# Spaces of 32 and 64 bytes between the late weight tiles of two mixture layers, in a matmul-bound kernel

## The chip, the cores and the metric

One core of one Trainium2 chip. The metric is the time of one execution on the device in microseconds (us); the times of several runs are given by their median.

## What is computed

Decayed linear attention over 2 x 8 heads x 768 positions, then a dense layer pair with g(h) = h * cos(h), then a mixture of eight experts with one expert for each token. Cut to what matters:

```python
x = np.ascontiguousarray(attn_out.transpose(0, 2, 1, 3)).reshape(B * S, H * D)   # 1536 x 512
h = x @ w_in                                                                     # 512 -> 2048
x = (h * np.cos(h)) @ w_out                                                      # 2048 -> 512
...
e_idx = np.argmax(x @ w_gate, axis=1)
for e in range(8):
    h = np.maximum(x[mask] @ w1[e], 0.0)                                         # 512 -> 1024
    out[mask] = gate_w[mask, None] * eom[mask, e, None] * (h @ w2[e])            # 1024 -> 512
```

## The kernel before, in words

All matrix products of the two layers run as products of float32r parts: a weight is split into a high and a low half (`hi`, `lo`), an activation likewise, and three products (high by high, high by low, low by high) are added in PSUM. The 1536 tokens are six blocks of 256. The hidden width of the dense layer is cut into eight pieces p = 0..7 of 256; an expert's into four.

The stages that matter here, with their lines:

- **First layer, `first`.** `mm_duo` (L511) multiplies two blocks at once: 12 matmuls with 512 moving columns for each half f of a piece; the weights `w_in` are the stationary operand and the tokens move. `mm_l1` (L499) does one block: 24 matmuls of 256 columns for a piece.
- **Second layer, `second`.** `mm_duo2` (L520) and `mm_l2` (L538): 12 matmuls of 512 columns each; here the activations `g` are stationary and the weights `w_out` move.
- **Order of the steps.** First come pieces 0 and 1 of blocks 0 to 2, beside the attention. Then for every p = 0..7 a step of the pair of blocks 3 and 4 in two halves and of block 5: L511, L520, L511, L520 or L538, L499 and so on. Then p = 2..7 for the pair of blocks 0 and 1 (12 half steps, L511 and L520), at last p = 2..7 of block 2 (L499 and L538).
- **Experts 0 and 1** are done in halves of 128 rows (`h_l1` L955, `h_l2` L982, both 512 columns, weights moving). **Experts 2 to 7** take 208 rows: `mm_rows` (L527 with 416 columns and L528 with 208, eight such pairs for a piece, weights stationary), `c_cols` (L904 with 416 and L906 with 208, eight pairs, weights stationary); expert 7 ends with L538.

**Where the weights lie.** `w_tile` gives the tile of a piece. Pieces 0 and 1 of `w_in` are the tile `wa01`; pieces 0 and 1 of `w_out` lie in the pool `wb`; pieces 2 to 7 lie in the pools `w2a` (`w_in`) and `w2b` (`w_out`), one tile of 8192 bytes per partition for each piece, kept for the whole kernel. The experts use the same tiles again: expert e takes places 0 to 3 or 4 to 7 of both pools (`place`), w1 in the first and w2 in the second. A pool gives out its addresses in the order in which its tags are first asked for: w7 first (by the loop on `spot`), then w2 to w6.

As built, a tile's first byte within 512 bytes is:

| tile | before | with the change |
|---|---|---|
| `wa01` (pieces 0, 1 of w_in), raw tiles | 320 | 320 |
| tokens `xs01`, `xs2`; activations `g`; pieces 0, 1 of w_out | 0 | 0 |
| w_in / w1 at places 7, 2, 3, 4, 5, 6 | all 0 | 32, 64, 96, 128, 192, 224 |
| w_out / w2 at places 7, 2, 3, 4, 5, 6 | all 0 | 224, 256, 288, 320, 352, 384 |

All slices of a weight tile that a matmul reads start at multiples of 512 bytes from the tile's start, so the table holds for each matmul's weights. PE, DVE and ACT run in the order of the program text (a manual schedule).

**The two small pools.** `sc` holds the row scales of the experts (`row_scale`, L745 to L767), `xt1` the single numbers of a rarely taken path at the end. Before, both are opened beside the weight pools and stay. `rt` and `xr` (routing) are closed in `routed` (L1003), where `rows` takes their place.

Of the kernel before, what the change touches and what calls it, by code (L numbers as in the profile page):

```python
# [8 lines left out]
F32 = mybir.dt.float32  # L9
F32R = mybir.dt.float32r  # L10
# [18 lines left out]
def kernel(  # L29
# [27 lines left out]
    NP = DFF // 256  # L57
# [18 lines left out]
    wb_p = ctx.enter_context(tc.tile_pool(name="wb", bufs=1))  # L76
# [56 lines left out]
    HP = 2  # L133
# [39 lines left out]
    pools = {}  # L173

    def w_load():
        i = nxt["load"]
        if i >= len(order) or (order[i][0] == "w1" and not pools.get("cleared")):
            return
        nxt["load"] += 1
        key = order[i]  # L180
        src = src_of[key[0]](*key[1:])
        words = key[0] in ("in", "out")
        pool, tag = (xt_p, "xt") if pools.get("spare") and i % 5 < 3 else (raw_p, "raw")
        if not pools.get("spare") and nxt["used"] < nxt["free"]:
            pool, tag = xt_p, "xt"
            nxt["used"] += 1
        if "raw2" in pools and i % 2:
            pool = pools["raw2"]
        if i in spot:
            t = spot[i]  # L190
        else:
            t = pool.tile([128, 1024], I32 if words else F32, tag=tag, name="raw")
            if pool is raw_p:
                in_raw.append(key)
        dst = t
        if len(src.shape) == 3:
            dst = t.rearrange("p (k f) -> p k f", k=src.shape[1])
        nc.sync.dma_start(out=dst, in_=src)
        raw_t[key] = t

    def w_tile(a, p, name):
        if a and p < HP:
            return wa01[:, p]
        pool = wb_p if p < HP else pools["w2a" if a else "w2b"]
        return pool.tile([128, 2, 1024], F32R, tag=f"w{p}", name=name)

    half_done, high_done = [], []
    spot, in_raw, used = {}, [], set()
# [13 lines left out]
    def word_parts():  # L222
# [7 lines left out]
        if f == 0:  # L230
            wt[name, p] = w_tile(name == "in", p, f"w_{name}_{p}")
# [343 lines left out]
    def behind(get, others):  # L575
        for x in others:
            tc.add_manual_dep(
                get.ins, x.name, mybir.DependencyInfo(mybir.DependencyClass.Sync, mybir.DependencyReason.DATA),
                reason="reads the scattered rows")
# [207 lines left out]
    def h_rows(t):  # L787
        for e in range(HALVED):
            if t == 0:
                r = cv_p.tile([128, ROW], F32, tag="x", name="hrows")  # L790
            else:
                if e == 0:
                    pools["h1"] = pools["rows"].tile([128, HALVED, ROW], F32, tag="rows", name="hrows")
                r = pools["h1"][:, e, :]
            r0 = e * CAP + t * 128
            behind(nc.sync.dma_start(out=r, in_=xs_d[r0:r0 + 128, :]), sent)
            rows[e, t] = r.unsqueeze(1)
# [16 lines left out]
    def c_rows(e):  # L814
        if e >= E:
            return
        t = pools["rows"].tile([128, 2, ROW], F32, tag="rows", name="rows")[0:HL]
        get = nc.sync.dma_start(
            out=t, in_=xs_d[(e + 1) * CAP - LIM:(e + 1) * CAP, :].rearrange("(t p) f -> p t f", p=HL))
        behind(get, sent)  # L820
        rows[e, 2] = t
# [17 lines left out]
    def c_high():  # L839
        i = nxt["split"]  # L840
        if i >= len(order):
            return
        nxt["split"] += 1
        key = order[i]
        r = raw_t.pop(key)
        t = w_tile(key[0] == "w1", place(*key), "w_" + "_".join(str(z) for z in key))
        nc.scalar.copy(out=t[:, 0, :], in_=r)  # L847
        low_due.append((t, r, key))
        wt[key] = t
# [145 lines left out]
    def totals():  # L995
        cps = side_tile([128, 512], "cps")
        nc.tensor.matmul(cps[:, 0:E], lhsT=ones, rhs=accoh, start=True, stop=True)
        nc.vector.tensor_add(out=cnt, in0=cps[:, 0:E], in1=skip[:, 0, :])
        nc.vector.tensor_scalar(more, cnt, float(127 - CAP), 0.0, ALU.add, ALU.max)
        nc.vector.tensor_scalar(more, more, 7, None, ALU.arith_shift_right)  # L1000
        nc.vector.tensor_reduce(out=most, in_=more, op=ALU.max, axis=AX.X)

    def routed():  # L1003
        totals()
        for c in reversed(rt_cms):
            c.__exit__(None, None, None)
        pools["rows"] = ctx.enter_context(tc.tile_pool(name="rows", bufs=2))
        h_rows(1)
        c_rows(HALVED)
        pools["spare"] = True  # L1010
        for _ in range(3):
            w_load()
# [101 lines left out]
    pools["side"] = ctx.enter_context(tc.tile_pool(name="ps_side", bufs=2, space=PSUM))  # L1114
    for nm, key in (("w2a", "w2a"), ("w2b", "w2b")):
        pools[key] = ctx.enter_context(tc.tile_pool(name=nm, bufs=1))
    pools["sc"] = ctx.enter_context(tc.tile_pool(name="scp", bufs=2))
    pools["xt1"] = ctx.enter_context(tc.tile_pool(name="xt1", bufs=1))
    pools["rt"], pools["xr"] = [c.__enter__() for c in rt_cms]
    WHOLE = NSB + 4 * HALVED  # L1120
    for z in range(4):
        if z % 2 == 0:
            t = pools[("w2a", "w2b")[z // 2]].tile([128, 2, 1024], I32, tag=f"w{NP - 1}", name="spot")
        spot[nxt["load"] + z] = t[:, z % 2]
    phase = tc.manual_schedule(engines={
# [142 lines left out]
    h_l1(H + 2, 1)  # L1268
    h_turn(H + 1)
    routed()  # L1270
    h_l2(H)
    convert_early(2)
# [44 lines left out]
    for i in range(WHOLE + 2, len(steps) + LAG):  # L1317
        e, p = divmod(i - WHOLE, EP)
# [73 lines left out]
    with tc.If(over > 0):  # L1392
# [13 lines left out]
        for e in range(E):  # L1406
            pos = pools["xt1"].tile([128, 1], F32, tag="pos", name="pos")
            nc.vector.tensor_copy(out=pos, in_=lane)
            n = nc.values_load(
                more[0:1, e:e + 1], min_val=0, max_val=limit, skip_runtime_bounds_check_because="counts of rows")  # L1410
# [33 lines left out]
```

## Time and profile before

| | |
|---|---|
| time, median of 3 runs | 522.54 us (522.42 to 523.0) |
| the profiled execution: its time | 523.34 us |
| its span, first to last instruction | 521.6 us |
| mean granted TensorE clock | 0.996 |
| PE / DVE / ACT / POOL busy | 98% / 66% / 61% / 19% of the span |
| DMA, mean over the span | 162 GB/s |

Matmuls overlap in the pipeline and their ends are modelled, so the duration of one says little; what a stream of them costs is read from the starts of its groups in the timeline: from the start of one group to the start of the next one.

### The profile page before, as it was taken

How to read it: one execution, taken by the hardware profiler on the slowest of the kernel's cores; microseconds unless marked ns; L12 is line 12 of the kernel's file. 1: busy time of each engine (PE TensorE's matmuls, PEld its weight loads, DVE VectorE, ACT ScalarE, POOL GpSimd, SP SyncE). 2: the span in 40 equal slices, each digit the busy share in tenths (PEclk: the TensorE clock that was granted, in tenths of full speed). 3: DMA queues.
4: the chain of work that ended last, by engine and by line, in shares of the span. 5: the costliest groups of instructions: out<-in, count | busy, mean ns of one | idle time of the engine just before them, and what ended most of it. 6: DMA issues, size and time to landing. Idle time of an engine off the chain costs nothing. (4 is left out here: it accounts for less than half of the span.)

```text
span 521.6 us, 8979 instructions
## 1 busy us (share of the span) xinstructions
PE 511.3 (98%) x3428; PEld 448.9 (86%) x3428; DVE 346.7 (66%) x672; ACT 317.3 (61%) x556; POOL 101.2 (19%) x129
## 2 busy tenths in 40 slices
PE   7989999999999999999999999999999999999995
PEld 7879988888888888887777888878889999999993
DVE  5897874577667566545554677756378888788740
ACT  3566655577666666655454665456577776777630
POOL 3454111132322323200102301311000011010111
PEclk9999999999999999999999999999999999999998
DMA  8999952232322423603912253658379777876311
GB/s 202 231 271 276 296 185 80 83 121 82 116 87 80 122 80 93 198 33 119 319 63 83 84 167 120 216 194 246 127 226 299 243 236 237 252 236 202 110 30 35
DMA packets 81938, 84.56 MB, mean 162 GB/s; under 512 B 41468, under 2 KB 61948, under 8 KB 81118
## 3 DMA queue, kind: packets, MB, share of 16 engines
q1 hardware_dynamic: 79646, 77.48, 49.3%
q0 software_dynamic: 2240, 6.42, 3.3%
q8 instruction: 29, 0.48, 0.4%
q14 instruction: 23, 0.19, 0.1%
HBM read 66.70 MB, written 17.65 MB: 162 GB/s over the span
## 5 line engine op out<-in xcount | busy, mean ns | idle before, releaser
L520 PE MATMUL acc<-w_out,g 128*128 128x512 f32 x336 | 82.3, 394 | 0.0
L520 PEld LDWEIGHTS acc<-w_out,g 128*128 128x128 f32 x336 | 61.7, 188 | 13.4 <-issue 1.2
L554 DVE SCALAR_TENSOR_TENSOR a<-a,t 128x512 f32<-128x512 f32 x48 | 34.6, 722 | 57.8 <-ACT a L551 57.8
L854 DVE TENSOR_TENSOR w_w<-raw,w_w 128x1024 fp32r<-128x1024 f32 x55 | 66.7, 1217 | 6.8 <-ACT w_w L847 6.7
L550 ACT ACTIVATE t<-h,quarter 128x512 f32<-128x512 f32 x48 | 33.0, 688 | 49.3 <-PE h L511 27.8
L847 ACT CAST w_w<-raw 128x1024 fp32r<-128x1024 f32 x55 | 57.6, 1054 | 2.2 <-DMA raw<-in_moe_w_dram 2.2
L538 PE MATMUL acc<-w_out,g 128*128 128x512 f32 x240 | 58.5, 394 | 0.0
L538 PEld LDWEIGHTS acc<-w_out,g 128*128 128x128 f32 x240 | 44.4, 188 | 9.6 <-issue 0.2
L904 PE MATMUL acc<-g,w_w 128*128 128x416 f32 x160 | 50.0, 371 | 0.0
L557 ACT ACTIVATE t<-a 128x512 f32<-128x512 f32 x48 | 30.3, 632 | 32.0 <-DVE a L554 32.0
L558 DVE TENSOR_TENSOR a<-t,h 128x512 f32<-128x512 f32 x48 | 33.0, 688 | 23.1 <-ACT t L557 21.0
L780 POOL DMA_INDIRECT out_dram<-y,who x16 | 16.1, 1005 | 148.2 <-ACT y L777 144.9
L527 PE MATMUL hw<-xs,w_w 128*128 128x416 f32 x144 | 44.7, 369 | 0.0
L561 ACT CAST g<-a 128x512 fp32r<-128x512 f32 x48 | 29.8, 621 | 23.8 <-DVE a L558 23.4
L562 DVE TENSOR_TENSOR g<-a,g 128x512 fp32r<-128x512 f32 x48 | 33.2, 692 | 16.5 <-ACT g L561 14.5
L906 PE MATMUL acc<-g,w_w 128*128 128x208 f32 x160 | 41.3, 258 | 0.0
L528 PE MATMUL hw<-xs,w_w 128*128 128x208 f32 x144 | 37.2, 258 | 0.0
L499 PEld LDWEIGHTS h<-xs,w_in 128*128 128x128 f32 x288 | 35.9, 191 | 1.1 <-issue 0.4
L499 PE MATMUL h<-xs,w_in 128*128 128x256 f32 x288 | 36.7, 284 | 0.0
L551 ACT ACTIVATE a<-t,magic 128x512 f32<-128x512 f32 x48 | 34.8, 725 | 1.6
L511 PE MATMUL h<-wa,w_in 128*128 128x512 f32 x144 | 35.2, 393 | 0.0
L268 POOL TENSOR_TENSOR w_out<-x,w_out 128x512 fp32r<-128x512 f32 x16 | 23.7, 1481 | 57.5 <-ACT w_out L262 56.8
(179 smaller groups left out, 1020.1 us busy)
## 6 DMA issues: line engine op xcount, KB each, us to landing
raw<-in_moe_w_dram SPq DMA_DIRECT2D x63, 512.0 KB, 4.5
raw<-in_moe_w_in_dram SPq DMA_DIRECT2D x14, 512.0 KB
raw<-in_moe_w_out_dram SPq DMA_DIRECT2D x14, 512.0 KB, 3.2
xs_d<-zrow SPq DMA_DIRECT2D x16, 266.0 KB, 4.3
x_d<-xrow SPq DMA_DIRECT2D x6, 532.0 KB
k<-in_k_dram SPq DMA_DIRECT2D x12, 256.0 KB, 6.8
q<-in_q_dram SPq DMA_DIRECT2D x12, 256.0 KB, 6.5
v<-in_v_dram SPq DMA_DIRECT2D x12, 256.0 KB
```

Of the source, the lines that this page charges most:

```text
L499: nc.tensor.matmul(h[:, f * n:(f + 1) * n], lhsT=wA(key, ws, kk, f), rhs=x[:, xx, kk, :], start=(z == 0), stop=(z == 3 * KD - 1))
L511: nc.tensor.matmul(h, lhsT=wA(key, ws, kk, f), rhs=x[:, :, xx, kk, :], start=(z == 0), stop=(z == 3 * KD - 1))
L520: nc.tensor.matmul(accs[t], lhsT=gf[:, gs, t * 128:(t + 1) * 128], rhs=wB(key, ws, f), start=(first and n == 0), stop=(last and n == 2))
L527: nc.tensor.matmul(h, lhsT=wA(key, 0, kk, f), rhs=x[:, kk], start=(kk == 0), stop=False)
L528: nc.tensor.matmul(h[:, 0, :], lhsT=wA(key, 1, kk, f), rhs=x[:, kk, 0, :], start=False, stop=(kk == KD - 1))
L538: nc.tensor.matmul(accs[t][0:m], lhsT=g[:, gs, f, t * m:(t + 1) * m], rhs=wB(key, ws, f), start=(first and n == 0), stop=(last and n == 5))
L551: nc.scalar.activation(out=a, in_=t, func=AF.Identity, bias=magic)
L554: nc.vector.scalar_tensor_tensor(out=a, in0=a, scalar=MAGIC, in1=t, op0=ALU.subtract, op1=ALU.subtract)
L847: nc.scalar.copy(out=t[:, 0, :], in_=r)
L854: nc.vector.tensor_sub(out=t[:, 1, :], in0=r, in1=t[:, 0, :].bitcast(F32))
L904: nc.tensor.matmul(acc, lhsT=wB(("w2", e, p), 0, f)[:, cols], rhs=g[:, :, f, :], start=(p == 0 and f == 0), stop=False)
L906: nc.tensor.matmul(acc[:, 0, :], lhsT=wB(("w2", e, p), 1, f)[:, cols], rhs=g[:, 0, f, :], start=False, stop=(p == EP - 1 and f == 1))
```

## The change

It asks the two pools for a small tile named `space` before the tile of a piece: 8 or 16 floats (32 or 64 bytes) per partition. Nothing reads or writes these tiles. So that all still fits, `sc` and `xt1` are opened after the routing pools are closed.

```diff
+    SHIFT_A = {7: 8, 2: 8, 3: 8, 4: 8, 5: 16, 6: 8}
+    SHIFT_B = {2: 8, 3: 8, 4: 8, 5: 8, 6: 8}
+    shifted = set()
+
+    def shift(a, p):
+        n = (SHIFT_A if a else SHIFT_B).get(p, 0)
+        if n and (a, p) not in shifted:
+            shifted.add((a, p))
+            pools["w2a" if a else "w2b"].tile([128, n], F32, tag=f"s{p}", name="space")
+
     def w_tile(a, p, name):
         if a and p < HP:
             return wa01[:, p]
-        pool = wb_p if p < HP else pools["w2a" if a else "w2b"]
-        return pool.tile([128, 2, 1024], F32R, tag=f"w{p}", name=name)
+        if p < HP:
+            return wb_p.tile([128, 2, 1024], F32R, tag=f"w{p}", name=name)
+        shift(a, p)
+        return pools["w2a" if a else "w2b"].tile([128, 2, 1024], F32R, tag=f"w{p}", name=name)
...
         pools["rows"] = ctx.enter_context(tc.tile_pool(name="rows", bufs=2))
+        pools["sc"] = ctx.enter_context(tc.tile_pool(name="scp", bufs=2))
+        pools["xt1"] = ctx.enter_context(tc.tile_pool(name="xt1", bufs=1))
         h_rows(1)
...
-    pools["sc"] = ctx.enter_context(tc.tile_pool(name="scp", bufs=2))
-    pools["xt1"] = ctx.enter_context(tc.tile_pool(name="xt1", bufs=1))
...
         if z % 2 == 0:
+            shift(z == 0, NP - 1)
             t = pools[("w2a", "w2b")[z // 2]].tile([128, 2, 1024], I32, tag=f"w{NP - 1}", name="spot")
```

On every engine and every queue the instructions and their order stay as they were; no instruction is added or taken away on them. What moves is a wait. On DVE, at the first expert's row scales (`h_scale(0, 0)`; `hrows` are that expert's rows, `ng` the first of the small tiles of `sc`, DMASW the queues of the indirect writes), there stood before:

```order
422 L854 TENSOR_TENSOR w_w_1_2_3866<-raw,w_w_1_2_3866 128x1024 [waits DMAHW5_49,Activation_49]
423 L972 TENSOR_TENSOR hg<-hT,hg 128x512 [waits Activation_49]
424 L854 TENSOR_TENSOR w_w_1_3_3887<-raw,w_w_1_3_3887 128x1024 [waits DMAHW0_49,Activation_49]
425 L755 TENSOR_SCALAR ng<-hrows 128x1 [waits DMAHW6_49]
426 L763 TENSOR_SCALAR sm<-sm 128x1 [waits Activation_49]
427 L764 TENSOR_SCALAR ez<-ez 128x1 [waits Activation_49]
```

and with the change:

```order
422 L866 TENSOR_TENSOR w_w_1_2_3877<-raw,w_w_1_2_3877 128x1024 [waits DMAHW5_49,Activation_49]
423 L984 TENSOR_TENSOR hg<-hT,hg 128x512 [waits Activation_49]
424 L866 TENSOR_TENSOR w_w_1_3_3898<-raw,w_w_1_3_3898 128x1024 [waits DMAHW0_49,Activation_49]
425 L767 TENSOR_SCALAR ng<-hrows 128x1 [waits DMASW3_49,DMASW2_49,DMAHW4_49,DMASW1_49,DMAHW6_49,DMASW0_49,Pool_49]
426 L775 TENSOR_SCALAR sm<-sm 128x1 [waits Activation_49]
427 L776 TENSOR_SCALAR ez<-ez 128x1 [waits Activation_49]
```

The wait for the last indirect writes of routing, which stood two row scales later, now stands at this first one, since `sc` lies where a buffer of `xr` lay. The same wait moves on ACT to the table load ahead of the first `ex`, and on POOL to the first write of rows to `out`.

## Rows read from the trace of the kernel before

**Rows 1.** The page, part 1: span, and PE's busy time.

```profile
span 521.6 us, 8979 instructions
PE 511.3 (98%) x3428; PEld 448.9 (86%) x3428; DVE 346.7 (66%) x672; ACT 317.3 (61%) x556; POOL 101.2 (19%) x129
```

**Rows 2.** Windows: stretch and length, busy time (instructions) of each engine, granted clock.

```profile
100.00:217.00 117.00, 117.00 (x599) 100.12 (x598) 77.83 (x129) 82.35 (x129) 32.69 (x24) 1.00 0.31 98
400.00:500.00 100.00, 100.00 (x691) 99.54 (x689) 81.25 (x159) 68.94 (x152) 8.02 (x8) 1.00 0.69 213
```

**Rows 3.** Timeline, PE, piece 6 of blocks 3 to 5: start us, length us, group.

```profile
186.13 2.91 PE L520 MATMUL acc<-w_out,g 128*128 128x512 f32 x12
188.88 2.88 PE L511 MATMUL h<-xs,w_in 128*128 128x512 f32 x12
191.60 2.88 PE L520 MATMUL acc<-w_out,g 128*128 128x512 f32 x12
194.32 2.88 PE L511 MATMUL h<-xs,w_in 128*128 128x512 f32 x12
197.04 2.88 PE L538 MATMUL acc<-w_out,g 128*128 128x512 f32 x12
199.76 3.04 PE L499 MATMUL h<-xs,w_in 128*128 128x256 f32 x24
202.63 0.63 PE L520 MATMUL acc<-w_out,g 128*128 128x512 f32 x2
```

**Rows 4.** Timeline, PE, piece 1 of the same blocks: weights in wa01.

```profile
97.84 2.96 PE L511 MATMUL h<-xs,wa 128*128 128x512 f32 x12
100.64 2.99 PE L499 MATMUL h<-xs,wa 128*128 128x256 f32 x24
103.47 0.86 PE L520 MATMUL acc<-w_out,g 128*128 128x512 f32 x3
```

**Rows 5.** Timeline, PE, first steps of blocks 0 and 1: tokens in wa01 move.

```profile
221.88 2.93 PE L511 MATMUL h<-wa,w_in 128*128 128x512 f32 x12
224.64 2.93 PE L520 MATMUL acc<-w_out,g 128*128 128x512 f32 x12
227.41 2.93 PE L511 MATMUL h<-wa,w_in 128*128 128x512 f32 x12
230.18 1.09 PE L538 MATMUL acc<-w_out,g 128*128 128x512 f32 x4
```

**Rows 6.** Groups by line, PE, whole span: names, count, busy us, mean ns.

```profile
L520 PE MATMUL acc<-w_out,g 128*128 128x512 f32 x336 | 82.3, 394 | 0.0
L511 PE MATMUL h<-wa,w_in 128*128 128x512 f32 x144 | 35.2, 393 | 0.0
L499 PE MATMUL h<-xs,w_in 128*128 128x256 f32 x288 | 36.7, 284 | 0.0
L982 PE MATMUL acc<-w_w,hg 128*128 128x512 f32 x96 | 24.0, 399 | 0.0
L527 PE MATMUL hw<-xs,w_w 128*128 128x416 f32 x144 | 44.7, 369 | 0.0
```

**Rows 7.** Timeline, PE, experts: eight pairs with w_w, then eight with wa.

```profile
405.50 0.37 PE L527 MATMUL hw<-xs,w_w 128*128 128x416 f32 x1
...
407.91 0.52 PE L803 MATMUL xps<-ident,rows 104*128 104x104 f32 x4
...
431.51 0.37 PE L527 MATMUL hw<-xs,wa 128*128 128x416 f32 x1
...
433.93 0.37 PE L904 MATMUL acc<-g,w_w 128*128 128x416 f32 x1
```

**Rows 8.** Line L847, ACT's writes of weight tiles: ns min/median/max, first and last start.

```profile
L847 ACT CAST w_w<-raw x55: 1031/1054/1077, 237.3 to 491.7; 128x1024 fp32r<-128x1024 f32 x55
L847 ACT CAST wa<-raw x8: 1031/1054/1074, 293.2 to 458.9; 128x1024 fp32r<-128x1024 f32 x8
```

**Rows 9.** Lines L796, L758 and L755: SP's row loads, ACT's table load, DVE's queue.

```profile
L796 SPq DMA_DIRECT2D hrows<-xs_d x4: 338/382/428, 331.9 to 357.1; - x4
L758 ACT ACT_TABLE_LOAD  x1: 1283/1283/1283, 358.1 to 358.1; - x1
L755 DVEq EVENT_SEMAPHORE  x3: 49/50/50, 372.7 to 372.9; - x3
```

## The prediction

> **What bounds the kernel now.** I read the page's busy times first. PE is busy for 511.3 of 521.6 us and DVE, the next, for 346.7 [rows 1]. The windows say the same of the stretches in which the late weight tiles are used: from 100 to 217 us and from 400 to 500 us PE is busy all the time and its clock is granted in full, while DVE and ACT have room [rows 2]. So the time of these stretches is the sum of the spacings of PE's matmuls, and a change of addresses counts if it changes a spacing. Only the timeline shows that: the start of a group to the start of the next one, over the matmuls in the group.
>
> The reader should then compare groups of the same line whose operands lie differently. In the steps of blocks 3 to 5 with pieces 2 to 7 every operand starts at 0 within 512 bytes. There a group of twelve 512-column matmuls takes 191.60 - 188.88 = 2.72 us, and so do the next three groups [rows 3], 226.7 ns for each matmul. Only the L520 group right behind the 24 small matmuls of L499 takes 2.75 (186.13 to 188.88), and the L499 group 2.87 (199.76 to 202.63). One step earlier in the program's order the same line L511 with the same tokens reads its stationary weights from `wa01`, at 320 within 512 bytes: 97.84 to 100.64, 2.80 us, 3% more; but L499 from the same tile takes 2.83 (100.64 to 103.47), 1.4% less [rows 4]. And where the tokens that move lie in `wa01` and the weights at 0, L511 takes 221.88 to 224.64, 2.76 us, and the L520 group behind it, with both operands at 0, does not fall back to 2.72 but takes 2.77; so does the pair after it, 227.41 to 230.18 being 2.77 [rows 5]. **So the relative place of the two operands does show in the spacing**, by a few hundredths of a microsecond for a group, both ways, and a group out of step leaves the next one slower. All-zero offsets give the shortest group of twelve that these rows hold.
>
> The rule that speaks against any effect: the Trainium skill, SBUF — State Buffer, section "SBUF: two separate sides", says that TensorE has its own ports and never waits on anyone, and TensorE: Matmul & The Clock Gate, "Step-by-step: what each phase is for", that loading the next weights takes no read bandwidth from the running matmul because there are two read ports. By that rule the sum below is 0. The trace disagrees: 2.80 against 2.72 us for one line with one tile exchanged.
>
> **The change, part by part.** *Adds and removes:* no instruction. The `space` tiles are never touched.
>
> *Blocks 3 to 5, pieces 2 to 7: six steps.* Each has two L511 groups, two L520 groups, one L538 group and one L499 group. L511 gets stationary weights off 0: 2.72 to 2.80, as in rows 4, +0.16 for two. L520 and L538 get moving weights off 0: the nearest row is a moving operand off 0 and what follows it, 2.77 [rows 5]; before they take 2.75 + 2.72 + 2.72 = 8.19 [rows 3], after 3 x 2.77 = 8.31, +0.12. L499: 2.87 to 2.83, -0.04. Together +0.24 a step, **+1.44 us** for six. I take these values because the rows are of the same lines; offset 320 is only one offset, and the new ones (32 to 384) are not in the trace. From below: only L511 pays, +0.12 a step, 0.72; from above: all five groups of twelve pay what L511 pays, 0.08, or (5 x 2.80) - (4 x 2.72 + 2.75) - 0.04 = 0.33 a step, 2.0.
>
> *Blocks 0 and 1: 24 groups of twelve* (144 matmuls of L511, as many of L520 [rows 6]). They run at 2.76 to 2.77 already, out of step because `wa01` moves [rows 5]. The new weights change one unlucky relation into another: **0**, with 0.04 a group either way (up to 2.80, or back to the aligned 2.72), 24 x 0.04 = 0.96 on both sides.
>
> *Block 2: six L499 groups and six L538 groups.* 6 x -0.04 = -0.24. The L538 groups stand behind other work and are not at 2.72 throughout; between 0 and +0.05 each I take 0.02, +0.12. Together **-0.1**.
>
> *Experts 0 and 1.* The moved places hold 12 of 16 tiles, so 72 of the 96 matmuls of L982 [rows 6] and as many of L955: twelve groups of twelve, again often restarted, +0.02 each: **+0.2** (0 to 0.6).
>
> *Experts 2 to 7.* Eight pairs of L527 and L528 take 405.50 to 407.91, 2.41 us, with weights at 0, and 431.51 to 433.93, 2.42, with weights at 320 [rows 7]. 144 / 8 = 18 such groups move [rows 6], and 15 groups of L904 and L906 (20 pieces, 5 of them in places that stay): 33 x 0.01 = **+0.3**. Nothing shows the pairs with other offsets; bounds are L499's -1.4% and L511's +3% of 2.41, or -0.03 and +0.07 a group: -1.0 to +2.3.
>
> *ACT, DVE and POOL write and read the tiles.* ACT's conversion takes 1054 ns in the median into the tiles at 0 and 1054 ns into `wa01` at 320 [rows 8]: nothing. Off 0 or not, these engines also have time left in both stretches [rows 2].
>
> *The moved wait.* The first row scale now waits for the last indirect writes. The row loads of SP at L796 wait for the same writes, and the last of them is issued at 357.1; ACT's table load, the first that would wait now, starts at 358.1 anyway [rows 9]. So the landing is covered by 1.0 us, and **0** is paid; what the queue spends on more semaphores (DVE: three of 50 ns, now earlier [rows 9]) is at most 0.2 us and only if PE waits for the hidden activations queued behind it on ACT. Without that cover the expert's first result and the next `hg` would come late by what the writes lack.
>
> Sum: 1.44 + 0 - 0.1 + 0.2 + 0.3 = **+1.8 us**. The profiled execution took 523.34 us, 0.80 over the median of the runs shown and 1.74 more than its span; it would go to 525.1. On the median, 522.54 + 1.8 = **524.3 us**. A measurement here can tell some 0.2% from no change, 1.05 us, so the bounds are 521.5 and 523.6. This case's own range is 523.6 to 526.0: the terms of the first stage between 0.7 and 2.0, the rest up to half their upper bounds.
>
> **The rivals.**
>
> *Spread offsets let the streams pass each other: faster.* Place: all matmuls with a moved operand. For it speaks L499, where a weight tile off 0 gains 1.4% [rows 3, 4]: with the operands at the same offset the loads and the stream may ask for the same place in turn, and 226.7 ns need not be the least possible spacing. Price at the same 1.4%: 30 groups of twelve in the first stage, 24, 6 and 12 in the others, 72 x -0.04 = -2.9; L499 12 x -0.04 = -0.5; expert pairs 33 x -0.03 = -1.0; in all -4.4, 518.1 us. If half the offsets are lucky, -2.2: **520.3 us**. It decides once the 72 groups, now 2.74 on average, come under 2.73, which with L499 is -1.2. Against it: neither L511 nor L520 shows a single group under 2.72, and the one stationary offset seen costs 3%.
>
> *Nothing, or gains and losses cancel: 522.5 us.* The new offsets give L499's gain (12 x -0.04 = -0.5, and the same from some others) against L511's loss. The two read ports of the Trainium skill, TensorE: Matmul & The Clock Gate, "Step-by-step: what each phase is for", would give the same time without any gain or loss. The changed offsets are multiples of 32 bytes; if only 320 were special and these offsets read like 0, all but L499 would stay at rows 3.
>
> *The moved wait bites: slower, by another way.* If the last writes land a microsecond later than before, ACT's table load and what is queued behind it shift by the same, and PE would wait for `hg`: under 1 us, 523 to 523.5. The cover of 1.0 us speaks against it [rows 9].
>
> *The change does not do what it says.* Excluded as built: the offsets are those asked for, the order of every engine is the same.
>
> **How the numbers follow.** The first stage slower as in rows 4 and 5: 0.44. Faster: 0.33, since one line of three gains by an offset and most new offsets are unseen. No change that can be told, with the late wait in it: 0.23. The range must reach both sides: 520.2, where the faster case has half its price, to 526.0, the upper end of the likeliest; about one in ten is left out below (the full price) and one in ten above.
>
> **What would show it.** In the profile after, the timeline of PE for pieces 2 to 7 of blocks 3 to 5: right if the L511 groups take 2.76 to 2.80 and the L520 groups 2.75 to 2.80, with L499 near 2.83 and a step 0.15 to 0.3 longer than the 16.5 us from one L520 group behind L499 to the next (186.13 to 202.63 [rows 3]). Wrong, to the fast side, if these groups show 2.70 or less; wrong to no change if they stay at 2.72. The table load of ACT should still start within 0.2 us of the conversion before it, and ACT's and DVE's durations should be the same. If the steps of blocks 0 and 1 move by more than 0.04 a group, the term that I set to 0 was the one that decided.

## The result and the profile after

The changed kernel takes 525.37 us in the median of five runs (524.99 to 526.95), the kernel before 523.0 (522.42 to 523.16) beside it: ratio 1.0054, 95% interval 1.0037 to 1.007. It is slower. The forecast was 524.3 us against a median of 522.54, which is a ratio of 1.0034, with 523.6 to 526.0 as the range of the slower case. Since the median of before moves between 523.0 and 523.7 from one comparison to another, ratios are compared below, not medians.

The page's first part of the kernel after, as [rows 1]:

```profile
span 523.6 us, 8978 instructions
PE 514.6 (98%) x3428; PEld 448.8 (86%) x3428; DVE 346.6 (66%) x672; ACT 317.3 (61%) x556; POOL 101.6 (19%) x129
```

PE's busy time grew by 3.3 us and its count did not change; DVE, ACT and POOL have the times of before. PE still has no gap to speak of, so the added time lies in the spacing of its matmuls.

To see where, cut both executions at the same matmuls: piece 1 of blocks 3 to 5 (L511, now L523), its piece 2, the first step of blocks 0 and 1, block 2's first, the first of experts 0 and 1, the expert pair of [rows 7], and the start of the last matmul. Windows of the kernel before (stretch and length, busy time and instructions of each engine, granted clock, DMA share, GB/s):

```profile
97.84:122.88 25.04, 25.04 (x134) 21.44 (x132) 16.51 (x27) 16.78 (x27) 6.10 (x4) 1.00 0.26 79
122.88:221.88 99.00, 99.00 (x506) 84.82 (x504) 64.30 (x107) 68.55 (x108) 27.87 (x21) 1.00 0.35 110
221.88:294.61 72.73, 72.68 (x359) 57.40 (x358) 37.02 (x89) 39.06 (x61) 6.82 (x10) 1.00 0.32 117
294.61:338.46 43.85, 43.85 (x293) 38.21 (x291) 32.06 (x70) 25.57 (x38) 9.26 (x12) 1.00 0.50 160
338.46:405.50 67.04, 67.04 (x373) 57.49 (x372) 43.03 (x97) 42.40 (x79) 7.26 (x7) 1.00 0.67 216
405.50:515.00 109.50, 109.50 (x729) 106.11 (x728) 80.26 (x159) 69.16 (x153) 11.01 (x11) 1.00 0.60 184
```

The same stretches of the kernel after:

```profile
97.26:122.30 25.04, 25.04 (x134) 21.45 (x133) 16.50 (x27) 16.79 (x27) 6.12 (x4) 1.00 0.23 81
122.30:222.68 100.38, 100.38 (x505) 84.59 (x504) 64.30 (x107) 68.51 (x108) 27.79 (x21) 1.00 0.33 108
222.68:296.01 73.33, 73.30 (x358) 57.43 (x357) 37.01 (x89) 39.08 (x61) 6.94 (x10) 1.00 0.32 116
296.01:339.93 43.92, 43.92 (x292) 37.96 (x291) 32.04 (x70) 25.52 (x38) 9.63 (x12) 1.00 0.49 160
339.93:407.38 67.45, 67.45 (x373) 57.53 (x372) 43.00 (x97) 42.47 (x79) 7.14 (x7) 1.00 0.66 214
407.38:517.09 109.71, 109.71 (x729) 106.13 (x728) 80.26 (x159) 69.29 (x153) 11.02 (x11) 1.00 0.60 183
```

The second column is the length. It grows by 0, 1.38, 0.60, 0.07, 0.41 and 0.21 us, 2.67 together, with PE busy throughout and its clock granted in full in both. The stretch ahead of 97.84, the attention, is 0.58 us shorter, so that the last matmul starts 515.00 to 517.09, 2.09 later. No matmul before that mark reads a tile that moved, and in the runs below that share this (the first five) the same matmul starts anywhere from 96.85 to 98.42 us. These 0.58 us are within that scatter, and a single span is worth no more than that. The stretches behind the mark repeat far better: in the first two runs below, which lose nothing, they add up to 417.08 and 417.09 us, before to 417.16.

PE's timeline after, piece 6 of blocks 3 to 5 (start us, length us, group), which answers to [rows 3]:

```profile
186.28 2.97 PE L532 MATMUL acc<-w_out,g 128*128 128x512 f32 x12
189.09 2.95 PE L523 MATMUL h<-xs,w_in 128*128 128x512 f32 x12
191.88 2.98 PE L532 MATMUL acc<-w_out,g 128*128 128x512 f32 x12
194.70 2.96 PE L523 MATMUL h<-xs,w_in 128*128 128x512 f32 x12
197.50 2.98 PE L550 MATMUL acc<-w_out,g 128*128 128x512 f32 x12
200.31 2.96 PE L511 MATMUL h<-xs,w_in 128*128 128x256 f32 x24
203.11 2.94 PE L532 MATMUL acc<-w_out,g 128*128 128x512 f32 x12
```

From one start to the next the groups take 2.81, 2.79, 2.82, 2.80, 2.81 and 2.80 us, where before they took 2.75, 2.72, 2.72, 2.72, 2.72 and 2.87. The step is 203.11 - 186.28 = 16.83 us against 16.50. In this step the weights of piece 6 of `w_in`, which stand, lie at 224 within 512 and those of piece 5 of `w_out`, which move, at 352 (the second layer runs one piece behind the first); in what follows such tiles are written `w_in_6` and `w_out_5`. Not every tile off 0 costs so much; the same timeline where `w_out_2` moves, which lies at 256:

```profile
136.22 2.91 PE L532 MATMUL acc<-w_out,g 128*128 128x512 f32 x12
138.97 2.97 PE L523 MATMUL h<-xs,w_in 128*128 128x512 f32 x12
141.77 2.44 PE L532 MATMUL acc<-w_out,g 128*128 128x512 f32 x10
```

L532 takes 2.75 here, what it took at 0. In blocks 0 and 1, as [rows 5]:

```profile
222.68 2.91 PE L523 MATMUL h<-wa,w_in 128*128 128x512 f32 x12
225.43 2.95 PE L532 MATMUL acc<-w_out,g 128*128 128x512 f32 x12
228.21 2.91 PE L523 MATMUL h<-wa,w_in 128*128 128x512 f32 x12
```

L523 takes 2.75 and no longer 2.76, L532 2.78 and no longer 2.77. `wa01` and `w_in_2` explain the first: `wa01` moves from 320 and `w_in_2` stands at 64, and 320 - 64 = 256. So two hints stand in this profile: it is the difference of the two addresses that counts, not each by itself, and 256 counts as 0.

The engines that write and read the tiles, and the moved wait: line L859 (L847 before, [rows 8]), and ACT's timeline around its table load [rows 9].

```profile
L859 ACT CAST w_w<-raw x55: 1032/1056/1069, 238.1 to 493.7; 128x1024 fp32r<-128x1024 f32 x55
L859 ACT CAST wa<-raw x8: 1035/1052/1081, 294.5 to 460.8; 128x1024 fp32r<-128x1024 f32 x8
```

```profile
358.59 1.06 ACT L859 CAST w_w<-raw 128x1024 fp32r<-128x1024 f32 x1
359.68 1.28 ACT L770 ACT_TABLE_LOAD   x1
```

The conversions last what they lasted, and the table load starts 0.03 us after the conversion ahead of it ends (358.59 + 1.06 = 359.65). The moved wait delays nothing.

### The profile page after: what moved, and what is told of

The parts are those of the page before. It is cut to its first block, busy times and chain, and to the rows that moved or that the text cites. A ratio compares the mean times of both kernels' runs of the same rounds, so it can differ in the third digit from the quotient of the medians.

```text
span 523.6 us, 8978 instructions
## 1 busy us (share of the span) xinstructions
PE 514.6 (98%) x3428; PEld 448.8 (86%) x3428; DVE 346.6 (66%) x672; ACT 317.3 (61%) x556; POOL 101.6 (19%) x129
## 5 line engine op out<-in xcount | busy, mean ns | idle before, releaser
L532 PE MATMUL acc<-w_out,g 128*128 128x512 f32 x336 | 83.2, 396 | 0.0
L532 PEld LDWEIGHTS acc<-w_out,g 128*128 128x128 f32 x336 | 61.7, 188 | 14.2 <-issue 1.2
L566 DVE SCALAR_TENSOR_TENSOR a<-a,t 128x512 f32<-128x512 f32 x48 | 34.6, 722 | 59.1 <-ACT a L563 59.0
L550 PE MATMUL acc<-w_out,g 128*128 128x512 f32 x240 | 59.0, 396 | 0.0
L859 ACT CAST w_w<-raw 128x1024 fp32r<-128x1024 f32 x55 | 57.6, 1053 | 2.2 <-DMA raw<-in_moe_w_dram 2.2
L550 PEld LDWEIGHTS acc<-w_out,g 128*128 128x128 f32 x240 | 44.4, 188 | 10.1 <-issue 0.2
L511 PEld LDWEIGHTS h<-xs,w_in 128*128 128x128 f32 x288 | 35.4, 188 | 1.2 <-issue 0.4
L511 PE MATMUL h<-xs,w_in 128*128 128x256 f32 x288 | 36.2, 281 | 0.0
L523 PE MATMUL h<-wa,w_in 128*128 128x512 f32 x144 | 35.4, 394 | 0.0
L523 PE MATMUL h<-xs,w_in 128*128 128x512 f32 x144 | 35.4, 395 | 0.0
```

The lines of the kernel that those rows point to most:

```text
L511: nc.tensor.matmul(h[:, f * n:(f + 1) * n], lhsT=wA(key, ws, kk, f), rhs=x[:, xx, kk, :], start=(z == 0), stop=(z == 3 * KD - 1))
L523: nc.tensor.matmul(h, lhsT=wA(key, ws, kk, f), rhs=x[:, :, xx, kk, :], start=(z == 0), stop=(z == 3 * KD - 1))
L532: nc.tensor.matmul(accs[t], lhsT=gf[:, gs, t * 128:(t + 1) * 128], rhs=wB(key, ws, f), start=(first and n == 0), stop=(last and n == 2))
L550: nc.tensor.matmul(accs[t][0:m], lhsT=g[:, gs, f, t * m:(t + 1) * m], rhs=wB(key, ws, f), start=(first and n == 0), stop=(last and n == 5))
L566: nc.vector.scalar_tensor_tensor(out=a, in0=a, scalar=MAGIC, in1=t, op0=ALU.subtract, op1=ALU.subtract)
```

## Theories and experiments

**Theory.** The spacing of PE's matmuls is set by the address of the weights that stand less the address of the rows that move, within 256 bytes. At a difference of 0 a group of twelve 512-column matmuls falls into the shortest spacing; at any other that the changed kernel has it is 1.3 to 3.5% longer. **Rivals:** the later pools and the moved wait cost something by themselves; it is the variety of offsets that counts; it is the distance from 0 within 512 bytes of either tile that counts.

### Only the later pools (e1_late_pools)

```diff
-    SHIFT_A = {7: 8, 2: 8, 3: 8, 4: 8, 5: 16, 6: 8}
-    SHIFT_B = {2: 8, 3: 8, 4: 8, 5: 8, 6: 8}
+    SHIFT_A = {}
+    SHIFT_B = {}
```

> Only the later opening of the two small pools is kept; no space between weight tiles, so every late weight tile lies at 0 within 512 bytes as before. Theory (the spacing of matmuls follows the relative place of their two operands within 256 bytes): nothing happens, 523.0 us, within 0.5 of the kernel before, and the L511 groups of blocks 3 to 5 (line numbers of before) stay at 2.72 us. Rival (the moved pools and the earlier wait cost the time): 525 us, with the whole loss kept, and groups of 2.72 us.

Measured: 523.21 us, ratio to before 0.9993 (0.9983 to 1.0003). The pools and the wait that moves with them cost nothing; the whole effect is in the spaces.

### All late tiles at 256 (e2_space256)

```diff
-    SHIFT_A = {7: 8, 2: 8, 3: 8, 4: 8, 5: 16, 6: 8}
-    SHIFT_B = {2: 8, 3: 8, 4: 8, 5: 8, 6: 8}
+    SHIFT_A = {7: 64}
+    SHIFT_B = {}
```

> The later pools, and one single space of 256 bytes ahead of the first late tile: all twelve late weight tiles lie at 256 within 512 bytes. Theory (the relation repeats every 256 bytes, since in the changed kernel the L520 groups with w_out at 256 fall back to 226.7 ns): 523.0 us, within 0.5 of before, groups of 2.72 us. Rival (the relation repeats only every 512 bytes, or any displacement of a weight tile from the other tiles costs): 1.5 to 2.5 us slower, 524.5 to 525.5, with L511 groups of 2.78 or more.

Measured: 523.29 us, ratio 0.9995 (0.9984 to 1.0007). PE's timeline, piece 6:

```profile
188.20 2.88 PE L523 MATMUL h<-xs,w_in 128*128 128x512 f32 x12
190.92 2.88 PE L532 MATMUL acc<-w_out,g 128*128 128x512 f32 x12
193.64 2.88 PE L523 MATMUL h<-xs,w_in 128*128 128x512 f32 x12
```

2.72 us for each group: twelve tiles off 0 within 512, and nothing of the loss. What counts repeats every 256 bytes.

### All late tiles at 96 (e7_space96)

```diff
-    SHIFT_A = {7: 8, 2: 8, 3: 8, 4: 8, 5: 16, 6: 8}
-    SHIFT_B = {2: 8, 3: 8, 4: 8, 5: 8, 6: 8}
+    SHIFT_A = {7: 24}
+    SHIFT_B = {}
```

> The later pools, and one single space of 96 bytes ahead of the first late tile: all late weight tiles at the same place, 96 within 512 bytes, so there are no six offsets, one difference only for each kind of matmul. Theory (the difference counts, not the variety): L511 of blocks 3 to 5 at difference 96, 2.81; L520 and L538 with weights moving, difference 160, 2.81; both as in the changed kernel's groups with these differences; L499 2.82; a step of blocks 3 to 5 +0.4, six +2.5, less 0.3 in block 2, +0.5 in blocks 0 and 1, +0.4 in the experts: 3.0 us slower than before, 526.0, and slower than the change by 0.6. Rival (tiles that lie alike are what is good, the spread over six offsets is what costs): 523.0.

Measured: 526.74 us, ratio 1.0064 (1.005 to 1.0078). Piece 6:

```profile
189.17 2.96 PE L523 MATMUL h<-xs,w_in 128*128 128x512 f32 x12
191.96 2.97 PE L532 MATMUL acc<-w_out,g 128*128 128x512 f32 x12
194.77 2.97 PE L523 MATMUL h<-xs,w_in 128*128 128x512 f32 x12
```

2.79 and 2.81 for these groups. There is no variety here, and the loss is no smaller than the change's: behind the attention the trace has 3.55 us more than before, where the change has 2.67. Against the run at 256 one number differs in the code, and the ratio goes from 0.9995 to 1.0064. A space by itself costs nothing, a wrong difference does.

### The first pool alone (e3_first_only), the second alone (e4_second_only)

`w_in` from 32 to 224 and all `w_out` at 256; then `w_in` at 0 and `w_out` from 224 to 384:

```diff
 # first pool alone
-    SHIFT_B = {2: 8, 3: 8, 4: 8, 5: 8, 6: 8}
+    SHIFT_B = {7: 8}
 # second pool alone
-    SHIFT_A = {7: 8, 2: 8, 3: 8, 4: 8, 5: 16, 6: 8}
-    SHIFT_B = {2: 8, 3: 8, 4: 8, 5: 8, 6: 8}
+    SHIFT_A = {}
+    SHIFT_B = {7: 56, 2: 8, 3: 8, 4: 8, 5: 8, 6: 8}
```

> The later pools, and the spaces of the change in the first pool alone (offsets 32 to 224); the second pool begins at 256 and holds all its tiles there. Theory: the first-layer weights cost, the second-layer weights cost only what it takes to fall back in step: L511 groups of blocks 3 to 5 at 2.78 to 2.81, L520 groups 2.73 to 2.75, L499 2.80 to 2.84; a step of blocks 3 to 5 +0.15, six of them +0.9; blocks 0 and 1 +0.3; block 2 -0.3; the experts +0.2; together +1.2, 524.2 us. Rival (each displaced tile costs alike, whatever it is read as): half of the whole loss in every stage, block 2 included.

> The later pools, and the spaces of the change in the second pool alone (offsets 224 to 384, as in the change); the first pool's tiles stay at 0. Theory: the L520 and L538 groups cost (2.76 at offset 320, 2.78 to 2.81 at 224, 288, 352 and 384, 2.72 to 2.75 at 256), the L511 groups with weights at 0 cost only the way back in step, 2.72 to 2.76, L499 stays at 2.87: blocks 3 to 5 +1.2, blocks 0 and 1 +0.3, block 2 +0.2, the experts +0.3; together +1.5 to +2.0, 524.5 to 525.0 us. Rival (only stationary weights matter, since they are what is loaded beside the stream): under 0.5 us slower.

Measured: 524.2 us, ratio 1.0023 (1.0011 to 1.0036), and 524.84, ratio 1.0025 (1.0014 to 1.0036). Piece 6 with the first pool alone, where the weights that stand are off:

```profile
188.85 2.95 PE L523 MATMUL h<-xs,w_in 128*128 128x512 f32 x12
191.65 2.89 PE L532 MATMUL acc<-w_out,g 128*128 128x512 f32 x12
194.37 2.95 PE L523 MATMUL h<-xs,w_in 128*128 128x512 f32 x12
```

and with the second alone, where the weights that move are off:

```profile
189.24 2.91 PE L523 MATMUL h<-xs,w_in 128*128 128x512 f32 x12
191.99 2.98 PE L532 MATMUL acc<-w_out,g 128*128 128x512 f32 x12
194.81 2.92 PE L523 MATMUL h<-xs,w_in 128*128 128x512 f32 x12
```

In the first L523 pays (2.80) and L532 stays at 2.72; in the second L532 pays (2.82), and L523 takes 2.75 because it begins out of step behind it. So each of the two operands pays in its own groups. The ratios add up to 1.0048, near 1.0054; by the traces behind the attention the two lose 1.29 and 1.76 us, together 3.05, more than the 2.67 of both at once. They need not add up exactly, since each alone also makes the groups that it leaves at a difference of 0 come back into step (L523 at 2.75 above).

### Everything in step (e5_aligned to e10_xs2_att): a gain that was lost elsewhere

If the difference is all that counts, the kernel before can be made faster: `wa01` lies at 320 = 64 within 256, so 64 bytes ahead of `xs01` bring the tokens, the activations and the other weights to 64 as well (e5_aligned).

```diff
+    cv_p.tile([128, 8], F32, tag="space", name="space")
     xs01 = xs_p.tile([128, 2, 2, KD, TB], F32R, tag="xs01", name="xs01")
```

(The pool has two buffers, hence 64 bytes.)

> The kernel before (small pools as before), with 64 bytes of space ahead of the tokens' tiles and nothing else: tokens, activations and all late weight tiles move together to 64 within 256 bytes, where the tile of pieces 0 and 1 (320, which is 64 within 256) already lies. Theory (only the difference of the two operands' places within 256 bytes counts): every matmul with 512 columns now has the difference 0 that only the late pieces of blocks 3 to 5 had; L511 with the tokens in wa01 goes from 2.76 to 2.72, the L511 groups of pieces 0 and 1 from 2.80 to 2.72, L520 behind them from 2.77 to 2.72-2.75; L499 of pieces 0 and 1 from 2.83 to 2.87; about 0.9 us faster than before, 522.1. Rival (a place other than 0 within 256 bytes costs by itself, whatever the other operand does): every late group slower, 525 us or more, L511 groups of 2.78 or more. A second rival (nothing is gained since these groups are restarted so often): 523.0.

Measured: 524.46 us, ratio 1.0028 (1.0016 to 1.0039): slower, a miss. But the timeline of blocks 0 and 1 shows what was meant:

```profile
223.76 2.88 PE L512 MATMUL h<-wa,w_in 128*128 128x512 f32 x12
226.48 2.88 PE L521 MATMUL acc<-w_out,g 128*128 128x512 f32 x12
229.20 2.88 PE L512 MATMUL h<-wa,w_in 128*128 128x512 f32 x12
```

2.72 us for groups that took 2.76 and 2.77 before [rows 5]; the whole stretch takes 72.12 us instead of 72.73, and behind the attention the kernel is 1.10 us ahead of before. Ahead of it, it has lost 2.08: piece 1 starts at 99.92 and not at 97.84.

A second kernel of this kind, e6_xs2, gave `xs2` (the second token tile: the tokens of block 5, then of block 2, later of the even experts) a pool of its own, at 352, so that the 256-column groups of L499 have a difference of 224 where they ran best (see the last section):

```diff
+    xs2_p = ctx.enter_context(tc.tile_pool(name="xs2", bufs=1))
...
+    xs2_p.tile([128, 8], F32, tag="space", name="space")
+    xs_p.tile([128, 8], F32, tag="space", name="space")
...
-        return xs_p.tile([128, 2, KD, TB], F32R, tag="xs2", name=name)
+        return xs2_p.tile([128, 2, KD, TB], F32R, tag="xs2", name=name)
```

(and the same pool for the two other tiles with that tag)

> As the aligned kernel with 64 bytes, but the second token tile (xs2, tokens of block 5 and block 2 in L499, of even experts in L527) lies 32 bytes past the others, so that weights minus tokens is 224 within 256 bytes for L499, the difference at which the changed kernel's L499 group took 2.80 us for 24 (116.7 ns each) against 120 at difference 0. Theory: L499 groups of late pieces 2.80 in place of 2.87, all groups of twelve at 2.72 to 2.75; 12 x -0.07 = -0.8 on top of the aligned kernel's -0.9: 521.3 us. Rival (L499's shorter spacing belongs to the place of the weights, not to the difference): L499 stays at 2.87 and the time at that of the aligned kernel, 522.1.

Measured: 524.42 us, ratio 1.0023 (1.0011 to 1.0035), again a miss with the same shape: 2.62 us lost ahead of piece 1, 1.51 gained behind it.

What was lost stands in the windows. From 10 to 38 us, the kernel before, then everything in step, then with `xs2` apart (last two columns: DMA share and GB/s):

```profile
10.00:38.00 28.00, 25.53 (x389) 22.57 (x390) 25.60 (x46) 14.48 (x26) 12.48 (x14) 1.00 1.00 248
```

```profile
10.00:38.00 28.00, 25.34 (x398) 22.08 (x394) 24.26 (x43) 13.50 (x23) 11.78 (x13) 1.00 1.13 233
```

```profile
10.00:38.00 28.00, 25.11 (x384) 21.59 (x382) 22.83 (x42) 13.18 (x23) 11.81 (x13) 1.00 1.08 228
```

The DMA engines are busy through most of this stretch in all three (the share adds up the times of the packets that start in it, and so can pass 1), and they move less in more time: 1.13/233 against 1.00/248 is 20% more engine time for a byte, 1.08/228 is 17% more. The space had pushed every pool behind it, the attention's among them, so that `q`, `k` and `v`, which are fetched in pieces of 64 floats (256 bytes), landed at 64 within 512 and no longer at 0. Two theories were left: the destinations of these transfers (A), or the difference of 0 in the L499 groups that run beside the attention (B). Three kernels tell them apart: the two above with 448 bytes of space at the start of the attention's pool, which put its tiles back to 0 (e8_aligned_att and e10_xs2_att), and the kernel before with 64 bytes there and nothing else (e9_att64).

```diff
     att = pools["att"].__enter__()
+    att.tile([128, 112], F32, name="space")
```

(with 16 in place of 112 in e9_att64)

> e5_aligned with 448 bytes of space ahead of everything in the attention's pool, so that q, k, v and the attention's other tiles lie at 0 within 512 again, as before, while all weights and activations stay at 64 (wa01 at 320). In e5_aligned the attention stage up to piece 1 got 2.08 us longer, and there the DMA engines moved 233 GB/s at a share of 1.13 against 248 GB/s at 1.00 before (10 to 38 us). Theory A (the destinations of q, k and v at 64 cost DMA time, and q and k come late): the DMA row goes back to some 248 GB/s at 1.00, the first L499-group goes back from 39.27 to 37.4 +- 0.6 us, and the whole is 522.3 (before 523.2, less 1.1 measured behind the attention in e5_aligned, plus some 0.2 for the 256-column groups of the attention at difference 0). Rival B (wa01 at difference 0 in the attention stage's own 256-column groups is what costs): 524.4, as e5_aligned.

> The kernel before with 64 bytes of space ahead of everything in the attention's pool and nothing else: only q, k, v and the attention's other tiles move, to 64 within 512. Theory A (their destinations cost DMA time): the DMA row of 10 to 38 us as in e5_aligned (about 233 GB/s at 1.1), q and k late, the first L499-group at 39 to 40 us instead of 37.4, and 525.2 (524.6 to 525.8) against 523.2. Rival B: no change, 523.2.

> e6_xs2 (weights at 64, wa01 at 320, xs2 at 352, so that L511, L520 and L538 groups have difference 0 everywhere and L499 groups with xs2 have 224) with the same 448 bytes ahead of the attention's tiles. Behind the attention e6_xs2 was 1.5 us ahead of the kernel before by its trace. Theory A: DMA row of 10 to 38 us as before, 521.7 to 522.0, faster than both kernels. Rival B: 524.4, as e6_xs2.

Measured, in that order: 522.41 us, ratio 0.9987 (0.9972 to 1.0001); 526.69 us, ratio 1.0055 (1.0037 to 1.0073); 521.97 us, **ratio 0.9964 (0.9951 to 0.9977)**. The windows from 10 to 38 us, in the same order:

```profile
10.00:38.00 28.00, 26.91 (x397) 23.70 (x396) 25.87 (x46) 14.69 (x26) 13.06 (x14) 1.00 1.04 254
```

```profile
10.00:38.00 28.00, 24.26 (x381) 21.01 (x380) 23.21 (x42) 13.50 (x23) 11.74 (x13) 1.00 1.07 227
```

```profile
10.00:38.00 28.00, 26.67 (x399) 23.25 (x396) 25.57 (x46) 14.18 (x26) 12.32 (x14) 1.00 1.02 245
```

With the attention's tiles back at 0 the DMA engines move 254 and 245 GB/s at 1.04 and 1.02; with those tiles alone at 64, 227 at 1.07. In the first, in which the L499 groups beside the attention keep the relation that B blames, piece 1 starts at 97.26, in the last at 97.90; before it was 97.84. The trace also has every packet of this stretch: those of 256 bytes, which are `q`, `k` and `v`, take 18.0 to 18.1 ns in the mean in all nine kernels that have these tiles at 0, and 21.6, 22.0 and 21.6 in the three that have them at 64 (e5_aligned, e6_xs2, e9_att64). Those of 1024 bytes show no such split (54.4 to 59.1 against 55.8 to 58.4); the few of 4 bytes slow down along with the 256-byte ones, from 9.0 ns to between 10.8 and 11.1. The second case shows who waits (PE's timeline, the middle of that stretch, in the brackets what ended the wait):

```profile
27.45 0.63 PE L387 MATMUL tkT<-ident,k 128*128 128x128 f32 x4 [1.04 <-DMA k<-in_k_dram]
28.33 0.63 PE L387 MATMUL tqT<-ident,q 128*128 128x128 f32 x4 [0.25 <-DMA q<-in_q_dram]
```

PE waits for `k` and `q`, 3.8 us in all ahead of piece 1 where before it waited 1.7, and piece 1 starts 2.77 us later than before; from there to the end this kernel runs as before to 0.03 us. Theory A holds and B falls; only the size for the 64 bytes alone was larger than the 2.0 us expected. The Trainium skill, DMA: Bandwidth & Descriptors, section "How a descriptor splits into AXI transactions", says that a transaction must start on a boundary of 256 bytes, so that a descriptor which does not begin on one starts at the boundary below it and pays for bytes that nobody uses; worked out by that rule, a 256-byte piece at 64 would be two transactions instead of one. That section puts the rule for what a transaction reads and does not say whether it holds for a destination. The trace, where a destination moved, goes in the same direction, with 17% more engine time for a byte; the number of transactions is not in it.

**The kernel with `xs2` apart and the attention's tiles at 0 is faster than both the kernel before and the changed one.** Behind the attention it is 1.46 us ahead of before: 0.35 in piece 1, 0.43 in pieces 2 to 7 of blocks 3 to 5, 0.59 in blocks 0 and 1 and 0.09 in the rest. The 0.43 stand in rows like these (piece 6):

```profile
196.46 2.88 PE L542 MATMUL acc<-w_out,g 128*128 128x512 f32 x12
199.18 2.96 PE L503 MATMUL h<-xs,w_in 128*128 128x256 f32 x24
201.98 2.91 PE L524 MATMUL acc<-w_out,g 128*128 128x512 f32 x12
```

The 512-column group stays at 2.72, and the 256-column group takes 2.80 instead of 2.87 [rows 3].

## Why the prediction was right, and where its terms were off

- **PE's spacing bounds these stretches, and the change pays there alone.** Right: in the six stretches above PE is busy all the time, ACT's, DVE's and POOL's times are those of before.
- **Blocks 3 to 5, pieces 2 to 7: +1.44, between 0.72 and 2.0.** Measured +1.38. The six steps, each from the first L532 group to the next one, take 16.67, 16.64, 16.80, 16.62, 16.83 and 16.77 us against 16.50: each within the 0.12 to 0.33 that the bounds gave it. But the step that took one price for all offsets was right on the average only, and that the average fits so well is luck: the prices came from a single offset, 320, and the 2.77 from rows whose difference was 192 and, behind them, 0. L523 takes 2.76 to 2.80, as forecast; L532 and L550, forecast at 2.77, take 2.74 to 2.75 with `w_out_2` (256), 2.76 with `w_out_4` (320), 2.78 to 2.82 with the others; in the first of the six steps they still read `w_out_1`, which did not move, and take 2.75. Their mean over the six steps is 2.77.
- **Blocks 0 and 1: 0, up to 0.96 either way.** Measured +0.60, the term that missed most. The step "one unlucky relation into another" failed. The relation before (moving from 320, standing at 0) is the mildest of all but 0: 2.76 for a group; the changed weights bring only `w_in_2` to a difference of 0 and give up the L520 groups, which had 0 in both operands. The prediction named this as the term that would decide if it moved; here it moved by 24 x 0.025 us, less than the 0.04 a group that was set as the sign.
- **Block 2: -0.1.** Measured +0.07. The gain of the 256-column groups was put too high and the loss of L538 too low: this stretch is 0.15 shorter with the first pool alone (forecast for these groups 0.24) and 0.24 longer with the second alone (forecast 0.12). **Experts 0 and 1: +0.2** (0 to 0.6). Measured +0.41. **Experts 2 to 7: +0.3** (-1.0 to +2.3). Measured +0.21. The pairs with 416 and 208 columns hardly feel the offsets: 0.21 of 109.50 us here, where two kernels without a loss differ from before by 0.09 and 0.08.
- **The moved wait: 0.** Right: the table load follows its predecessor by 0.03 us, and the later pools alone give 0.9993.
- **The sum: +1.8.** The traces give +2.67 behind the attention, the timed ratio 2.8 us of 523.0, the two medians 2.4. The difference to the traces is the term for blocks 0 and 1, and 0.2 for each of block 2 and experts 0 and 1. The upper end of the range does not follow from its own words: 2.0 for the first stage and half the upper bounds of the rest, 0.48, 0.3 and 1.15, are 3.9, which is 526.5 and not 526.0. The measured time lies below both.
- **The rival "faster by spread offsets"** falls for 512 columns: at eight differences no group is under 2.72, and one difference of 96 for all late tiles gives 1.0064. Its one ground, L499's gain, is real (L511 took 2.80 to 2.85 after), but is 24 short matmuls in a step against 60 long ones.
- **The rival "nothing"** falls: from 256 to 96, with everything else equal, the ratio goes from 0.9995 to 1.0064. Its ground that other offsets may read like 0 holds, of those tried, for 256 bytes only, or where both operands move alike (e5_aligned).

## What to carry to other kernels

Where PE is busy without a gap, compare the start-to-start time of equal groups whose operands lie differently, and try the difference of the two addresses, not each offset: here 512-column fp32r matmuls wanted it to be 0 within 256 bytes. A space that repairs this moves every pool behind it; keep the destinations of transfers in 256-byte pieces where they were, or the gain is lost there. When a kernel that should be faster is not, cut it at the same instructions before giving up the theory: the gain was in the trace both times.

## What was not expected of the hardware

- **Spacing by difference.** From the starts of the groups of blocks 3 to 5, start of a group to start of the next one over twelve: mean spacing of a 512-column matmul with (standing less moving) within 256 bytes of 0, in the kernel before: 226.7 ns; in the kernel after, of 192: 229.6 to 230.4; 128: 231.2 to 232.7; 224: 231.9 to 233.2; 32: 232.6 to 233.3; 64: 233.2; 96: 234.0; 160: 234.2 to 234.6. It is nearly the same number whether the weights stand at 192 and the tokens move from 0 (229.6), or the weights move from 320 and what stands lies at 0 (230.0 to 230.4; both 192).
- **The other way round for 256 columns.** There a difference of 0 is the worst of those seen: 119.7 ns for a group of 24, against 118.8 at 128, 118.5 at 32, 117.8 at 64, 117.5 at 192, 117.4 at 96 and 116.7 at 224. This is why L499 gained where L511 lost, and why `xs2` apart pays.
- **A group falls into step by itself, but not at once.** Behind other work a group with difference 0 runs 233, 236, 228, 233, 231 ns and then 227 throughout; this is why the first L520 group of a step takes 2.75 and not 2.72, and why a group with difference 0 behind one without it takes up to 2.76.
- **Destinations at 64** cost 17 to 20% more engine time for a byte over a stretch that is mostly transfers in 256-byte pieces, as the windows above show; the 256-byte packets themselves take 18.0 to 18.1 ns at 0 and 21.6 to 22.0 at 64.

What inside PE or its memory makes the difference of the addresses count stays open; the runs show the relation, not its cause. That the transfers' cost also repeats every 256 bytes was not tried, nor were other offsets for them than 0 and 64.
